# Distance bias of an attention kernel: a bias of all tiles but the first made by distance and read back skewed from memory, with a changed beginning

## The chip, the cores and the metric

The kernel runs on one core of a Trainium2 chip. The metric is the device time of one execution in microseconds (us). Its engines, by the names of the profile: PE (TensorE, matmuls; PEld its weight loads), DVE (VectorE), ACT (ScalarE), POOL (GpSimd) and SP (SyncE, which here only issues DMAs). A matmul writes to PSUM, whose buffers are the tiles of the pools ps_s, ps_t and ps_x.

## The reference

Attention with a learned distance bias, then two layers on its output, all in float32. B = 2, H = 8 heads, S = 576 positions, D = 64.

```python
scores = q @ k.T / sqrt(D)
x = log1p(abs(i - j)) / log1p(max(i, 1))        # for rows i, columns j
h = relu(x * w1 + b1)                           # 32 hidden values for every (i, j)
bias = h @ w2                                   # one value per head
attn = softmax(scores + bias)                   # over j
out = attn @ v                                  # heads side by side: 1152 x 512
y = ((out @ w_a) * (out @ w_b)) @ w_out         # 512 -> 1536 -> 512
z = y @ w_in                                    # 512 -> 1024
z = layernorm(z * softmax(z)) * g_ln
result = z @ w_out2                             # 1024 -> 512
```

## The kernel before

The attention goes over tiles of 128 rows of scores, all 576 columns at once: tiles 0 to 3 for each of the two batches, and a fifth unit that holds the last 64 rows of both batches. That makes nine units of eight heads, 72 steps. What a step does is written out in the string `ORDER`, one letter per part, at the loop near the end of the attention; `later(n, f)` and the tables `SECOND_T`, `LAST_T`, `KEYS` put other work into step n. No scheduler changes that order: each engine does its instructions as they are written. The first tile's bias is made before step 0. From about 207 us the two layers follow, which the change does not touch; some of their work already stands in the last units.

A step does, for one head: `scores` (PE, four matmuls `s<-kst,qhi` and `qlo`), `biased` (DVE, L417: adds the bias, writes `e` and the row maximum `nm`), `exp` (ACT, L424, with the row sum), `rec` (POOL, L428, then DVE, L433, its reciprocal), `shares` (POOL, L434, scales `e`), `turned` (PE transposes `e` into `pt`, L442; DVE or ACT copies it into `et`, L447 and L445) and `values` (PE, L471, into `px`). In the course of a unit Q and K for later ones are transposed (`tp_q`, `tp_k`), and split into a high and a low part (`qhi` on ACT, `qlo` on DVE, L325), as is the output (`xhi`, and `xlo` on DVE, L482).

The bias is made in 36 groups T of 16 rows. x*w1 = log1p(|i-j|)*w1/log1p(i), so one table `tabs` of log1p(distance)*w1 serves all rows: relu(a*x + b) = a*relu(x + b/a), with a = 1/log1p(i). For a group, four tiles `h` of 128 partitions (4 rows by 32 hidden values) by 576 columns are a window of the table, plus a number per partition, and no less than 0 (`bias_hidden`, L354 on DVE, L356 on ACT; which of the two is in the strings `HIDDEN`, "v" or "a"). `bias_sums` (L364) multiplies each with w2 into 32 partitions of PSUM, in two halves of 288 columns, four column groups of PE side by side. `bias_out` (L374) copies the sums (16 rows by 8 heads) with the factor a into `st`, and `bias_sent` (L383) has SP send them as rows into `bias_t`, [128 rows, 8 heads, 576]. `place(T)` gives tile and rows of T.

The table is made on PE (L209, into ps_s buffers), its right part first, the left part during the first tile's groups. `ps_s` has two buffers, shared by the table, the sums `bps` and the scores `s`. Dummy matmuls (`beside`, L405) stand in the steps 2 and 3.

Of the kernel before, what the change touches and what calls it, by code (L numbers as in the profile page):

```python
# [17 lines left out]
P = 128  # L18
# [36 lines left out]
def tile_kernel(ctx, tc, q, k, v, w1, b1, w2, w_a, w_b, w_out, w_in2, w_out2, g_ln, psi, rpsi, out):  # L55
# [14 lines left out]
    OFF = S - 4  # L70
    KD = DM // P
# [92 lines left out]
    with ExitStack() as actx:  # L164
# [7 lines left out]
        sp = actx.enter_context(tc.tile_pool(name="sp", bufs=4))  # L172
        ps_t = actx.enter_context(tc.tile_pool(name="ps_t", bufs=3, space=PSUM))
# [3 lines left out]
        tabs = ac.tile([P, UW + NG], F32, name="tabs")  # L177
        w2bd = ac.tile([P, 4 * H], F32, name="w2bd")
        rp = ac.tile([P, NG // 4], F32, name="rp")
        tb, nb = tabs[:, 0:UW], tabs[:, UW:].rearrange("p (c k) -> p c k", c=4)  # L180
        low = OFF - (S - 1 - 12)
        half = OFF - (P - 1 - 12)

        right, left, raw = (ep.tile([P, 2 * S], F32, tag="e", name=n) for n in ("psi_r", "psi_l", "raw"))
# [355 lines left out]
        for w in second[1:]:  # L540
# [3 lines left out]
            if w == second[3]:  # L544
                scores(0, 1)
# [451 lines left out]
```

## Time and profile before

| | |
|---|---|
| median of 3 runs | 546.56 us (546.26 to 547.12) |
| the profiled execution's own time | 544.4 us |
| its span in the trace | 542.6 us |
| busy: PE, DVE, ACT, POOL | 531.1, 418.9, 286.9, 156.3 us |
| first `biased` (step 0) | 28.73 us after the span's start |
| units 0 and 1 from step 3 on | 34.57 to 72.30 us |
| units 2 to 5 | 72.30 to 147.29 us |
| units 6 and 7 | 147.29 to 183.39 us |

The span is what the trace covers; the execution's time is 1.8 us more. A unit is cut at the start of its first `biased`. PE is busy nearly all of the span, in the attention with the matmuls of the scores, the bias and the values. Matmuls of four column groups run side by side, and each shows its own record, so the sum of their durations is not the time that PE spends on them; that is read from the starts of what comes before and after.

### The profile page before, as it was taken

How to read it: one execution, taken by the hardware profiler on the slowest of the kernel's cores; microseconds unless marked ns; L12 is line 12 of the kernel's file. 1: busy time of each engine (PE TensorE's matmuls, PEld its weight loads, DVE VectorE, ACT ScalarE, POOL GpSimd, SP SyncE). 2: the span in 40 equal slices, each digit the busy share in tenths (PEclk: the TensorE clock that was granted, in tenths of full speed). 3: DMA queues.
4: the chain of work that ended last, by engine and by line, in shares of the span. 5: the costliest groups of instructions: out<-in, count | busy, mean ns of one | idle time of the engine just before them, and what ended most of it. 6: DMA issues, size and time to landing. Idle time of an engine off the chain costs nothing.

```text
span 542.6 us, 12408 instructions
## 1 busy us (share of the span) xinstructions
PE 531.1 (98%) x4880; PEld 472.3 (87%) x4880; DVE 418.9 (77%) x903; ACT 286.9 (53%) x599; POOL 156.3 (29%) x262
## 2 busy tenths in 40 slices
PE   7899999999999999999999999999999999999997
PEld 3487788888878899999999999999999988888886
DVE  5788889999885795897899798897884467656661
ACT  5779987788786663555564334522534332232321
POOL 2034445555455630222222122242224330000000
PEclk9999999999999999999999999999999999999999
DMA  4895433333266012544554353444300000000011
GB/s 97 184 216 127 112 86 85 79 71 81 69 153 181 3 41 70 166 135 138 155 147 126 117 156 116 125 147 145 125 5 2 0 1 20 21 19 21 19 30 48
DMA packets 53917, 49.32 MB, mean 91 GB/s; under 512 B 31582, under 2 KB 44131, under 8 KB 53860
## 3 DMA queue, kind: packets, MB, share of 16 engines
q1 hardware_dynamic: 53584, 48.52, 33.1%
q8 instruction: 38, 0.62, 0.5%
q14 instruction: 19, 0.16, 0.1%
q10 hardware_dynamic: 276, 0.02, 0.0%
HBM read 34.37 MB, written 2.36 MB: 68 GB/s over the span
## 4 chain that ended last, share of the span: by engine, by line
PE 89%; DVE 5%; issue 2%; ACT 2%; POOL 1%; DMA 0%; SPq 0%; ACTq 0%; DVEq 0%; POOLq 0%
PE pm L132 27%; PE po L132 14%; PE py L894 9%; PE ph L834 9%; PE bps L364 7%; PE s L398 6%; PE px L471 6%; PE pt L442 5%; DVE e L417 2%; PE tp_k L288 1%; PE pl L875 1%; PE tp_q L288 1%; ACT e L424 1%; PE table L209 1%; DVE et L447 1%
## 5 line engine op out<-in xcount | busy, mean ns | idle before, releaser
L102 POOL TENSOR_SCALAR f<-f 128x512 f32<-128x512 f32 x48 | 41.2, 860 | 138.3 <-ACT f L98 128.6
L132 PE MATMUL pm<-xhi,abh 128*128 128x384 f32 x240 | 80.2, 334 | 0.0
L132 PE MATMUL pm<-xhi,abl 128*128 128x384 f32 x240 | 80.2, 334 | 0.0
L132 PE MATMUL pm<-xlo,abh 128*128 128x384 f32 x240 | 80.2, 334 | 0.0
L424 ACT ACTIVATE e<-e,nm 128x576 f32<-128x576 f32 x72 | 56.0, 778 | 29.8 <-DVE nm L417 28.4
L434 POOL TENSOR_SCALAR e<-e,rec 128x576 f32<-128x576 f32 x72 | 54.1, 751 | 28.8 <-DVE rec L433 26.7
L417 DVE CUSTOM_DVE_ANT_0 e<-s,bias 128x576 f32<-128x576 f32 x72 | 53.9, 750 | 2.4 <-PE s L398 0.8
L354 DVE TENSOR_SCALAR h<-tabs 128x576 f32<-128x576 f32 x115 | 54.6, 515 | 0.1
L151 ACT COPY one<-pm 128x384 f32<-128x384 f32 x36 | 17.3, 480 | 60.2 <-PE pm L132 60.2
L132 PE MATMUL po<-gh,oh 128*128 128x384 f32 x144 | 48.5, 337 | 0.6 <-DVE x2s L765 0.6
L364 PE MATMUL bps<-h,w2bd 128*32 128x288 f32 x576 | 46.0, 420 | 2.9 <-ACT st L374 1.6
L132 PE MATMUL po<-gh,ol 128*128 128x384 f32 x144 | 48.4, 336 | 0.0
L132 PE MATMUL po<-gl,oh 128*128 128x384 f32 x144 | 48.4, 336 | 0.0
L442 PE MATMUL pt<-ident,e 128*128 128x128 f32 x288 | 45.1, 279 | 0.9 <-POOL e L434 0.9
L132 PEld LDWEIGHTS pm<-xhi,abh 128*128 128x128 f32 x240 | 45.0, 188 | 0.0
L132 PEld LDWEIGHTS pm<-xhi,abl 128*128 128x128 f32 x240 | 45.0, 188 | 0.0
L132 PEld LDWEIGHTS pm<-xlo,abh 128*128 128x128 f32 x240 | 45.0, 188 | 0.0
L428 POOL TENSOR_SCALAR rec<-sums 128x1 f32<-128x1 f32 x72 | 21.0, 292 | 80.5 <-ACT e L424 80.2
L114 DVE SCALAR_TENSOR_TENSOR f<-words,f 128x512 int32<-128x512 int32 x48 | 42.5, 885 | 1.6
L398 PE MATMUL s<-kst,qhi 128*128 128x288 f32 x160 | 40.6, 335 | 1.2 <-DVE nm L417 1.2
L471 PE MATMUL px<-et,vsb 128*32 128x128 f32 (+1 forms) x1280 | 40.4, 264 | 0.0
L442 PEld LDWEIGHTS pt<-ident,e 128*128 128x128 f32 x288 | 32.8, 140 | 8.7 <-POOL e L434 3.7
(137 smaller groups left out, 1251.2 us busy)
## 6 DMA issues: line engine op xcount, KB each, us to landing
bias<-st SPq DMA_DIRECT2D x40, 288.0 KB, 3.6
words<-in_moe_w_out_dram SPq DMA_DIRECT2D x20, 512.0 KB, 3.6
words<-in_moe_w_a_dram SPq DMA_DIRECT2D x12, 512.0 KB, 3.7
words<-in_moe_w_b_dram SPq DMA_DIRECT2D x12, 512.0 KB, 3.5
words<-in_moe_w_in_dram SPq DMA_DIRECT2D x8, 512.0 KB, 3.7
nat_q<-in_q_dram SPq DMA_DIRECT2D x16, 128.0 KB, 3.2
arena_hi<-in_k_dram SPq DMA_DIRECT2D x16, 128.0 KB, 2.6
vsb<-in_v_dram SPq DMA_DIRECT2D x16, 128.0 KB, 2.8
```

What stands on the lines that cost most here:

```text
L114: nc.vector.scalar_tensor_tensor(out=b, in0=words[:, :, 0], scalar=29, in1=b, op0=ALU.logical_shift_right, op1=ALU.bitwise_or)
L132: nc.tensor.matmul(ps, w, x, start=(i == 0), stop=(i == n - 1))
L354: nc.vector.tensor_scalar(h, win, sc, 0.0, op0=ALU.add, op1=ALU.max)
L364: nc.tensor.matmul(bps[32 * qd:32 * qd + 32, a, 0:SH], w2bd, h[:, a * SH:(a + 1) * SH], start=True, stop=True)
L398: nc.tensor.matmul(ps[:, a, 0:SH], w, kst[:, b, h, a * SH:(a + 1) * SH], start=(m == 0), stop=(m == len(mm) - 1))
L417: nc.vector.tensor_tensor_reduce(out=halves(e), in0=ps[:, :, 0:SH], in1=halves(bias_t[it][:, h, :]), op0=ALU.add, op1=ALU.min, scale=1.0, ...
L424: nc.scalar.activation(e, e, AF.Exp, bias=nm, scale=-1.0, accum_out=sums[:, h:h + 1])
L434: nc.gpsimd.tensor_scalar(e, e, rec[:, h:h + 1], 1.0, op0=ALU.mult, op1=ALU.mult)
L442: nc.tensor.transpose(pt[:, c, :], e[:, j * TL + c * P:j * TL + (c + 1) * P], ident)
L471: nc.tensor.matmul(px[rows, p, cols], lhsT, rhs, start=(c == 0 and m == 0), stop=(c == NC), skip_group_check=True)
L834: nc.tensor.matmul(ph[u][:, a], x[:, kc, cols], w[:, kc, a * 512:(a + 1) * 512], start=(i == 0), stop=(i == 3 * KD - 1))
L894: nc.tensor.matmul(ps, x[:, c, :], w[:, c, cols], start=(i == 0), stop=(i == 3 * KF - 1))
```

## The change

The bias depends on the column only through the distance |i-j|, apart from the row's own numbers. For all groups T of 8 and up, `h` is now made over distances 0 to d-1 and no longer over columns: d = max(before + 1, behind), where before = t0 + 60 columns can lie ahead of the group's rows and behind = S - t0 behind them. d is 319 to 384 in tile 2, 381 to 448 in tile 1, 445 to 512 in tile 3, and 573 to 576 in the last one. `bias_sums` has one matmul per `h` where there were two (two if d is over 512). `bias_out` copies the sums into `st` of 636 columns in two pieces, the distances behind the row as they are and those ahead of it read backwards. SP writes `st` to a tile `bd` in memory (`bias_sent`), and one step later reads it back into `bias_t` with a skewed address pattern, four columns further to the left for each next four rows (`bias_in`, the new part "m" of a step). The first tile still has its bias made by columns, its sums split at 512 and 64 where they were 288 and 288.

The tiles are taken in the order 0, 2, 1, 3, 4. `h` of tiles 1 to 3 is all made on DVE (`HIDDEN`); before, ACT made some of it. The groups of the second tile come at other steps (`SECOND_T`), those of the later tiles two steps earlier, the last ones too (`LAST_T`). In the beginning, the second part of the table (now distances 0 to 575, 288 columns in each of two pieces) is made in ps_t buffers and no longer in ps_s, and its load `psi_l` is gone; the last two pieces of K and the Q of the second half of the heads are transposed in step 2, behind the scores of step 1; `beside` of step 2 is 2 matmuls where it was 9; the loads of V for the second batch come two steps earlier.

```diff
-ORDER = {0: "kbvioljpatsxu", 2: "kbvioljptsxu", 3: "kbglfviojptshaxu", 4: "khbvioljpatsxu", 55: "khbilospajtvxu"}
+ORDER = {0: "kbvimoljpatsxu", 2: "kbvimoljptsxu", 3: "kbglfvimojptshaxu", 4: "khbvimoljpatsxu", 55: "khbilmospajtvxu"}
...
-SECOND_T = (5, 7, 9, 10, 12, 13, 14)
-LAST_T = (48, 50, 52, 54)
-HIDDEN = (("vvva", "vvva", "vvva", "vvva", "vvva", "vvva", "vvva", "vava"),
-          ("vvvv", "avvv", "avav", "avvv", "avav", "avvv", "avav", "avvv"), ("vvvv", "avvv"))
+SECOND_T = (5, 6, 8, 9, 10, 11, 12)
+LAST_T = (46, 48, 50, 52)
+TILES = (0, 2, 1, 3, 4)
+HIDDEN = (("vvva", "vvva", "vvva", "vvva", "vvva", "vvva", "vvva", "vvva"),
+          ("vvvv",), ("vvvv",), ("vvvv",), ("vvvv", "avvv"))
...
+        dp = actx.enter_context(tc.tile_pool(name="dp", bufs=4, space=bass.MemoryType.DRAM))
...
-        def table(a, n, row, at):
-            ps = ps_s.tile([P, 2, 512], F32, tag="s", name=f"table_{a}")
+        def table(n, at, step, pool, tag):
             w = (n + 1) // 2
+            halves = []
             for i in range(2):
                 m = min(w, n - i * w)
+                ps = pool.tile([P, 512], F32, tag=tag, name=f"table_{step}_{i}")
                 for g in range(4):
-                    o = a + i * w - 4 * g - at
-                    nc.tensor.matmul(ps[g * HID:(g + 1) * HID, i, 0:m], w1r, row[:, o:o + m], start=True, stop=True)
-            return [(tb[:, a + i * w:a + min(n, (i + 1) * w)], ps[:, i, 0:min(w, n - i * w)]) for i in range(2)]
-        halves_r = table(half, UW - half, psi_r, half - 12)
+                    o = at + i * w - step * g
+                    nc.tensor.matmul(ps[g * HID:(g + 1) * HID, 0:m], w1r, psi_d[:, o:o + m], start=True, stop=True)
+                halves.append((tb[:, i * w:i * w + m], ps[:, 0:m]))
+            return halves
+        halves = table(NX, 12, 4, ps_s, "s")
...
+        def reach(T):
+            _, it, r, c = place(T)
+            t0 = it * P + r + c
+            return t0 + 60, S - t0
         def bias_hidden(T, quads=range(4)):
-            it, r, c = place(T)
+            n, it, r, c = place(T)
+            before, behind = reach(T)
             for qd in quads:
                 t0 = it * P + r + 16 * qd
-                h = hp.tile([P, S], F32, tag="h", name=f"h_{T}_{qd}")
-                win = tb[:, OFF - t0 - c:OFF - t0 - c + S]
+                a, d = (OFF - half - t0 - c, S) if n == 0 else (0, max(before + 1, behind))
+                h = hp.tile([P, S], F32, tag="h", name=f"h_{T}_{qd}")[:, 0:d]
+                win = tb[:, a:a + d]
                 sc = nb[:, c, t0 // 16:t0 // 16 + 1]
-                if HIDDEN[min(it, 2)][T % len(HIDDEN[min(it, 2)])][qd] == "v":
+                if HIDDEN[n][T % len(HIDDEN[n])][qd] == "v":
                     nc.vector.tensor_scalar(h, win, sc, 0.0, op0=ALU.add, op1=ALU.max)
                 else:
                     nc.scalar.activation(h, win, AF.Relu, bias=sc)
...
         def bias_sums(T):
-            bps = ps_s.tile([P, 2, 512], F32, tag="s", name=f"bps_{T}")
+            bps = ps_s.tile([P, 2, 512], F32, tag="s", name=f"bps_{T}").rearrange("p a j -> p (a j)")
             for qd, h in enumerate(bias_w[T]):
-                for a in range(2):
-                    nc.tensor.matmul(bps[32 * qd:32 * qd + 32, a, 0:SH], w2bd, h[:, a * SH:(a + 1) * SH], start=True, stop=True)
+                d = h.shape[1]
+                for a in range(0, d, 512):
+                    cols = slice(a, min(d, a + 512))
+                    nc.tensor.matmul(bps[32 * qd:32 * qd + 32, cols], w2bd, h[:, cols], start=True, stop=True)
             bias_w[T] = bps
-        def bias_out(T, send=True):
-            it, r, c = place(T)
+        def bias_rows(T):
+            _, it, r, c = place(T)
             if it not in bias_t:
                 bias_t[it] = big.tile([P, H, S], F32, tag="big", name=f"bias_{it}")
-            st = stp.tile([P, S], F32, tag="st", name=f"st_{T}")
+            return [bias_t[it][base + c:base + 64:4] for base in ((r,) if it < NC else (0, TL))]
+        def bias_out(T, send=True):
+            n, it, r, c = place(T)
+            before, behind = reach(T)
+            st = stp.tile([P, W], F32, tag="st", name=f"st_{T}")
+            bps = bias_w.pop(T)
             k = 9 * c + 2 * it + r // 64
-            nc.scalar.activation(st.rearrange("p (a j) -> p a j", a=2), bias_w.pop(T)[:, :, 0:SH], AF.Copy, scale=rp[:, k:k + 1])
+            if n == 0:
+                nc.scalar.activation(st[:, 0:S], bps[:, 0:S], AF.Copy, scale=rp[:, k:k + 1])
+                for rows in bias_rows(T):
+                    nc.sync.dma_start(rows, st[:, 0:S])
+                return
+            nc.scalar.activation(st[:, before:W], bps[:, 0:behind], AF.Copy, scale=rp[:, k:k + 1])
+            nc.scalar.activation(st[:, 0:before], bps[:, before:0:-1], AF.Copy, scale=rp[:, k:k + 1])
             bias_w[T] = st
             if send:
                 bias_sent(T)
         def bias_sent(T):
-            it, r, c = place(T)
-            st = bias_w.pop(T)
-            for base in ((r,) if it < NC else (0, TL)):
-                nc.sync.dma_start(bias_t[it][base + c:base + 64:4], st)
+            st, bias_w[T] = bias_w[T], dp.tile([P, W], F32, tag="bd", name=f"bd_{T}")
+            nc.sync.dma_start(bias_w[T], st)
+        def bias_in(T):
+            bd = bias_w.pop(T)[:, :]
+            for rows in bias_rows(T):
+                nc.sync.dma_start(rows, bass.AP(bd.tensor, bd.offset + 60, [[8 * W - 4, 16], [W, 8], [1, S]]))
...
-        units = [(it, [b]) for it in range(NC) for b in range(B)] + [(NC, list(range(B)))]
+        units = [(it, [b]) for it in TILES[:NC] for b in range(B)] + [(TILES[NC], list(range(B)))]
...
-        nc.sync.dma_start(psi_l, psi[3:4, low + 3 - 12:half + 3])
...
-                halves_l = table(low, half - low, psi_l, low - 12)
+                halves = table(S, 12 + OFF - half, 0, ps_t, "t")
...
-            turn(w)
-            keep_high(w)
-            if w == second[3]:
-                scores(0, 1)
-        later(2, beside, 9)
+            if w in second[:4]:
+                turn(w)
+                keep_high(w)
+        scores(0, 1)
+        for w in second[4:] + second[:1]:
+            later(2, turn, w)
+            keep_at.setdefault(3, []).append(w)
+        later(2, beside, 2)
         later(3, beside, 3)
+        later(3, keep_low, second[0])
         later(1, bias_sent, N0)
-        later(1, turn, second[0])
-        later(2, keep_high, second[0])
-        low_at[3] = [second[0]]
+        in_at[4] = [N0]
...
-            later(7 + p, load_v, 1, p)
+            later(5 + p, load_v, 1, p)
...
-            n = LAST_T[r] if i == NC - 1 else 16 * i + (SECOND_T[r - 1] if i == 0 else 2 * r)
+            n = LAST_T[r] if i == NC - 1 else SECOND_T[r - 1] if i == 0 else 16 * i - 2 + 2 * r
...
+            in_at.setdefault(n + 2, []).append(T)
...
+                if part == "m":
+                    for T in in_at.get(n, []):
+                        bias_in(T)
```

The rows below are the programs' instructions in their order, engine by engine, with the names that the code gives and a buffer number. First SP in units 0 and 1, the queue that issues the DMAs, before; `bias_1` is the bias of the second tile, T = 11 to 15:

```order
L383 DMA bias_1_422<-st_11_898 16x8x576
L334 DMA vsb_161<-in_v_dram 128x4x64 x2
L383 DMA bias_1_422<-st_12_978 16x8x576
L383 DMA bias_1_422<-st_13_1084 16x8x576
L257 DMA nat_q_2_1_0_1102<-in_q_dram 128x4x64
L383 DMA bias_1_422<-st_14_1121 16x8x576
L383 DMA bias_1_422<-st_15_1188 16x8x576
```

And the same groups after, where `bd` is the tile in memory and `bias_2` the bias of the tile that is now the second:

```order
L410 DMA bd_11_866<-st_11_863 128x636
L263 DMA nat_q_2_0_0_891<-in_q_dram 128x4x64
L416 DMA bias_2_560<-bd_11_866 16x8x576
L410 DMA bd_12_915<-st_12_912 128x636
L416 DMA bias_2_560<-bd_12_915 16x8x576
L410 DMA bd_13_996<-st_13_993 128x636
L416 DMA bias_2_560<-bd_13_996 16x8x576
L410 DMA bd_14_1045<-st_14_1042 128x636
L416 DMA bias_2_560<-bd_14_1045 16x8x576
L410 DMA bd_15_1104<-st_15_1101 128x636
L263 DMA nat_q_2_1_0_1121<-in_q_dram 128x4x64
L416 DMA bias_2_560<-bd_15_1104 16x8x576
```

Each group now has two DMAs on SP, and the next group's write stands behind the read of this one.

Next DVE in unit 2, around the step that also has `xlo` of the unit ahead, before:

```order
L417 ISA nm_2_3_1390 128x1
L482 TENSOR_TENSOR xlo_1021<-px_1_801,xhi_1020 128x4x128
L447 COPY et_2_1_1401<-pt_2_1_1396 128x512
L354 TENSOR_SCALAR h_19_1_1414<-tabs_104 128x576
L433 RECIPROCAL rec_2_1229<-rec_2_1229 128x1
L417 ISA e_2_4_1427,nm_2_4_1428<-s_2_4_1407,bias_1_422 128x576
L417 ISA nm_2_4_1428 128x1
L354 TENSOR_SCALAR h_19_2_1470<-tabs_104 128x576
L354 TENSOR_SCALAR h_19_3_1472<-tabs_104 128x576
```

And after:

```order
L450 ISA nm_2_3_1394 128x1
L515 TENSOR_TENSOR xlo_1039<-px_1_806,xhi_1038 128x4x128
L480 COPY et_2_1_1406<-pt_2_1_1401 128x512
L368 TENSOR_SCALAR h_20_0_1417<-tabs_106 128x384
L368 TENSOR_SCALAR h_20_1_1419<-tabs_106 128x384
L466 RECIPROCAL rec_2_1237<-rec_2_1237 128x1
L450 ISA e_2_4_1428,nm_2_4_1429<-s_2_4_1412,bias_2_560 128x576
L450 ISA nm_2_4_1429 128x1
L368 TENSOR_SCALAR h_20_2_1473<-tabs_106 128x384
L368 TENSOR_SCALAR h_20_3_1475<-tabs_106 128x384
```

Every step has two `h` there now, of fewer columns, where some steps had one; and the group is one further on.

Last PE in the beginning, from the table's second part on, before:

```order
L209 MATMUL table_9_344<-psi_l_108,psi_r_107 32x224 x8
L364 MATMUL bps_5_353<-h_5_0_308,w2bd_105 32x288 x2
L364 MATMUL bps_5_353<-h_5_1_310,w2bd_105 32x288 x2
...
L398 MATMUL s_0_1_457<-kst_160,qhi_0_0_0_213 128x288 x2
L398 MATMUL s_0_1_457<-kst_160,qlo_0_0_0_214 128x288 x2
L288 MATMUL tp_k_0_1_3_464<-ident_72,arena_lo_164 128x128 x4
L288 MATMUL tp_k_0_1_4_472<-ident_72,arena_lo_164 128x64 x4
L288 MATMUL tp_q_0_1_0_502<-ident_72,nat_q_0_1_0_182 128x128 x4
L398 MATMUL s_0_2_512<-kst_160,qhi_0_0_0_213 128x288 x2
```

And after:

```order
L214 MATMUL table_0_0_346<-logs_109 32x288 x4
L214 MATMUL table_0_1_351<-logs_109 32x288 x4
L380 MATMUL bps_5_356<-h_5_0_310,w2bd_107 32x512
L380 MATMUL bps_5_356<-h_5_0_310,w2bd_107 32x64
...
L431 MATMUL s_0_1_460<-kst_163,qhi_0_0_0_215 128x288 x2
L431 MATMUL s_0_1_460<-kst_163,qlo_0_0_0_216 128x288 x2
L431 MATMUL s_0_2_495<-kst_163,qhi_0_0_0_215 128x288 x2
L431 MATMUL s_0_2_495<-kst_163,qlo_0_0_0_216 128x288 x2
L294 MATMUL tp_k_0_1_3_500<-ident_72,arena_lo_167 128x128 x4
L294 MATMUL tp_k_0_1_4_505<-ident_72,arena_lo_167 128x64 x4
L294 MATMUL tp_q_0_1_0_510<-ident_72,nat_q_0_1_0_184 128x128 x4
```

The table has 288 columns in place of 224, the sums are split at 512, and two pieces of K and the Q stand behind the scores of step 2.

## Rows read from the trace of the kernel before

**Rows 1.** The page: the span, and busy time by engine.
```profile
span 542.6 us, 12408 instructions
...
PE 531.1 (98%) x4880; PEld 472.3 (87%) x4880; DVE 418.9 (77%) x903; ACT 286.9 (53%) x599; POOL 156.3 (29%) x262
```

**Rows 2.** Busy time by stretch, with granted clock and DMA share.
```profile
core 0: us, PE busy (x) PEld busy (x) DVE busy (x) ACT busy (x) POOL busy (x), PEclk, DMA share, GB/s
34.57:72.30 37.73, 37.55 (x544) 29.34 (x546) 33.26 (x93) 32.25 (x70) 14.69 (x30) 1.00 0.57 130
72.30:90.78 18.48, 18.48 (x300) 15.45 (x296) 17.22 (x45) 14.85 (x34) 9.36 (x18) 1.00 0.34 81
90.78:109.66 18.88, 18.88 (x321) 15.92 (x316) 17.32 (x46) 15.35 (x34) 9.63 (x19) 1.00 0.33 78
...
128.14:147.29 19.15, 19.03 (x323) 16.02 (x318) 17.29 (x46) 15.30 (x34) 9.62 (x19) 1.00 0.33 77
147.29:166.43 19.14, 18.35 (x279) 15.27 (x270) 15.07 (x41) 14.67 (x33) 8.75 (x18) 1.00 0.63 146
```

**Rows 3.** Timeline of PE: start, duration, operation, tiles, and number of records.
```profile
89.59 1.20 PE L364 MATMUL bps<-h,w2bd 128*32 128x288 f32 x16
90.59 1.08 PE L471 MATMUL px<-et,vsb 128*32 128x128 f32 x32
```

**Rows 4.** Timeline of a step with a copy and two `h`.
```profile
93.04 0.76 DVE L417 CUSTOM_DVE_ANT_0 e<-s,bias 128x576 f32<-128x576 f32 x1
...
93.73 0.69 DVE L447 COPY et<-pt 128x512 f32<-128x512 f32 x1
...
93.84 0.78 ACT L424 ACTIVATE e<-e,nm 128x576 f32<-128x576 f32 x1 [0.69 <-DVE nm L417]
...
94.33 0.94 DVE L354 TENSOR_SCALAR h<-tabs 128x576 f32<-128x576 f32 x2
...
94.79 0.52 POOL L428 TENSOR_SCALAR rec<-sums 128x1 f32<-128x1 f32 x1 [0.74 <-ACT e L424]
...
95.47 0.76 DVE L417 CUSTOM_DVE_ANT_0 e<-s,bias 128x576 f32<-128x576 f32 x1
```

**Rows 5.** Timeline of a step of unit 7, which makes no bias.
```profile
170.62 0.74 DVE L417 CUSTOM_DVE_ANT_0 e<-s,bias 128x576 f32<-128x576 f32 x1
...
172.41 0.19 POOL L428 TENSOR_SCALAR rec<-sums 128x1 f32<-128x1 f32 x1 [0.58 <-ACT e L424]
...
172.75 0.76 DVE L417 CUSTOM_DVE_ANT_0 e<-s,bias 128x576 f32<-128x576 f32 x1
```

**Rows 6.** Instructions by line and form up to 208 us.
```profile
line engine op names shapes xcount | busy us, mean ns | idle before us <-releasers
L354 DVE TENSOR_SCALAR h<-tabs 128x576 f32<-128x576 f32 x115 | 54.6, 515 | 0.1
...
L275 DVE TENSOR_SCALAR arena_lo<-arena_hi 128x256 fp32r<-128x256 f32 x8 | 2.3, 284 | 0.0
L102 DVE TENSOR_SCALAR single<-single 128x512 f32<-128x512 f32 x4 | 1.7, 416 | 0.0
```

**Rows 7.** Timeline of the beginning; idle time before in brackets.
```profile
17.25 0.96 PE L209 MATMUL table<-psi_l,psi_r 1*32 1x224 f32 x16
...
20.27 1.20 PE L364 MATMUL bps<-h,w2bd 128*32 128x288 f32 x16 [0.55 <-ACT st L374]
...
22.50 1.20 PE L364 MATMUL bps<-h,w2bd 128*32 128x288 f32 x16 [1.03 <-ACT st L374]
...
23.80 0.74 ACT L374 ACTIVATE st<-bps,rp 128x576 f32<-128x576 f32 x1 [1.11 <-PE bps L364]
...
28.73 0.76 DVE L417 CUSTOM_DVE_ANT_0 e<-s,bias 128x576 f32<-128x576 f32 x1 [0.39 <-DMA arena_hi<-in_k_dram]
```

**Rows 8.** Timeline: `biased` of the steps 9 and 16.
```profile
51.79 0.74 DVE L417 CUSTOM_DVE_ANT_0 e<-s,bias 128x576 f32<-128x576 f32 x1
...
72.30 0.76 DVE L417 CUSTOM_DVE_ANT_0 e<-s,bias 128x576 f32<-128x576 f32 x1 [0.25 <-PE bps L364]
```

**Rows 9.** DMA issues: KB each, median us from issue to landing.
```profile
bias<-st SPq DMA_DIRECT2D x40, 288.0 KB, 3.6
...
out_dram<-osb SPq DMA_DIRECT2D x7, 256.0 KB, 2.0
```

More of the change, by code (lines that the diff above doesn't have):

```diff
@@ L70, in tile_kernel @@
     OFF = S - 4
+    W = S + 60
     KD = DM // P
@@ L172, in tile_kernel @@
         sp = actx.enter_context(tc.tile_pool(name="sp", bufs=4))
+        dp = actx.enter_context(tc.tile_pool(name="dp", bufs=4, space=bass.MemoryType.DRAM))
         ps_t = actx.enter_context(tc.tile_pool(name="ps_t", bufs=3, space=PSUM))
         ps_x = actx.enter_context(tc.tile_pool(name="ps_x", bufs=1, space=PSUM))
-        tabs = ac.tile([P, UW + NG], F32, name="tabs")
+        half = OFF - (P - 1 - 12)
+        NX = UW - half
+        tabs = ac.tile([P, NX + NG], F32, name="tabs")
         w2bd = ac.tile([P, 4 * H], F32, name="w2bd")
         rp = ac.tile([P, NG // 4], F32, name="rp")
[L180 to L184, printed above, removed]
+        tb, nb = tabs[:, 0:NX], tabs[:, NX:].rearrange("p (c k) -> p c k", c=4)
+        logs, at_i, raw = (ep.tile([P, 2 * S], F32, tag="e", name=n) for n in ("logs", "psi_i", "raw"))
         w2r, rp_in = raw[:, 0:H], raw[:, H:H + NG // 4]
-        nr_, nl_ = UW - half + 12, half - low + 12
-        psi_r, w1r, b1r = (right[0:1, o:o + n] for o, n in ((0, nr_), (nr_, HID), (nr_ + HID, HID)))
-        psi_l, psi_i = left[0:1, 0:nl_], left[0:1, nl_:nl_ + 4 * NG].rearrange("p (c t) -> p c t", c=4)
+        psi_d, w1r, b1r = (logs[0:1, o:o + n] for o, n in ((0, NX + 12), (NX + 12, HID), (NX + 12 + HID, HID)))
+        psi_i = at_i[0:1, 0:4 * NG].rearrange("p (c t) -> p c t", c=4)
         warm = ac.tile([P, 1], F32, name="warm")
-        nc.sync.dma_start(psi_r, psi[0:1, half - 12:UW])
+        nc.sync.dma_start(psi_d, psi[0:1, half - 12:UW])
         nc.sync.dma_start(w1r, w1)
@@ L215, in tile_kernel @@
             nc.tensor.matmul(ps_nb[g * HID:(g + 1) * HID], b1r, psi_i[:, :, g::4], start=True, stop=True)
-        nc.scalar.copy(*halves_r[0])
+        nc.scalar.copy(*halves[0])
         nc.vector.tensor_copy(nb, ps_nb)
-        nc.vector.tensor_copy(*halves_r[1])
+        nc.vector.tensor_copy(*halves[1])
         for g in range(4):
@@ L482, in inputs_low @@
             nc.vector.tensor_tensor(out=xlo, in0=px, in1=xhi.bitcast(F32), op=ALU.subtract)
-        units = [(it, [b]) for it in range(NC) for b in range(B)] + [(NC, list(range(B)))]
+        units = [(it, [b]) for it in TILES[:NC] for b in range(B)] + [(TILES[NC], list(range(B)))]
         qs = {}
-        extra, sums_at, out_at, keep_at, low_at = {}, {}, {}, {}, {}
+        extra, sums_at, out_at, in_at, keep_at, low_at = {}, {}, {}, {}, {}, {}
         def later(n, f, *args):
@@ L515, in tile_kernel @@
             if T == N0:
-                nc.scalar.copy(*halves_l[0])
-                nc.vector.tensor_copy(*halves_l[1])
+                nc.scalar.copy(*halves[0])
+                nc.vector.tensor_copy(*halves[1])
             if T <= N0:
@@ L633, in tile_kernel @@
             for part in ORDER[max(i for i in ORDER if i <= n)]:
-                if part == "o":
+                if part == "m":
+                    for T in in_at.get(n, []):
+                        bias_in(T)
+                elif part == "o":
                     for T in out_at.get(n, []):
```

4 lines of the change are left out of this document (2 added, 2 removed).

## The prediction

> **What bounds the kernel now.** I read the page first: TensorE is busy 531.1 of 542.6 us [rows 1]. That share does not say what a removed TensorE instruction is worth, so I cut the attention, which is all the change touches, into its units of eight steps at the starts of `biased`, and read the busy time by stretch [rows 2]. In the units from 72.30 to 128.14 TensorE is busy all of the time, while VectorE has 17.2 of 18.5 us and ScalarE 15. Then I read one step in order of time. A step's softmax is a ring that runs once per step: VectorE adds the bias and takes the row maximum, ScalarE takes the exponential, GpSimd turns the sum, VectorE inverts it, and only then comes the next `biased`. With nothing in the way that ring takes 172.75 - 170.62 = 2.13 us [rows 5]. Where VectorE has a copy of `et` and two `h` to do, the ring is longer: the copy starts at 93.73, the two `h` at 94.33, they end at 95.27, and GpSimd's small `rec`, ready at 94.79, takes 0.52 there in place of 0.19 and ends 0.04 behind them; the next `biased` starts at 95.47, a step of 2.43 [rows 4]. So the reader is to see two chains of nearly one length: TensorE's sum of work and this ring. Work taken from TensorE alone gives at most what the ring also gives back.
>
> The ring and TensorE don't bound the beginning; there the bias of the first tile does. The sums of T = 6 and 7 wait 0.55 and 1.03 us for ScalarE to free a buffer, the copy of T = 7 starts at 23.80, and the first `biased` at 28.73, when its bias rows have landed [rows 7].
>
> **The change part by part.** All against the profiled execution's 544.4 us (span 542.6). The median of the three runs shown is 546.56, 2.2 above it; the sum of differences is carried over to the median.
>
> *Widths of `h`.* One `h` of 576 columns has an interval of 0.94 - 0.51 = 0.43 behind another [rows 4, 6]. The mean duration is 515 ns at 576, and of the same form 416 at 512 (L102) and 284 at 256 (L275) [rows 6]. The last two give 0.52 ns per column, so I take intervals of 0.295 us at 320 columns, 0.327 at 383, 0.36 at 447 and 0.393 at 510. The form is the same, tensor_scalar on VectorE, so both ends are near.
>
> *Widths of the sums.* Sixteen matmuls of 288 columns, four column groups side by side, keep TensorE from 89.59 until the next kind of work starts at 90.59 [rows 3]: 1.0, of which I take 0.97 as paid by columns, 1.68 ns for each of 576. One matmul of d columns in each group then costs 0.54 (d = 319), 0.64 (382), 0.75 (447) and 0.86 (510). No row shows a matmul of 320 to 512 columns in this form; the bounds are proportional to columns (these) and no gain (0.97).
>
> *A, the beginning.* The table's second half takes no ps_s buffer any more, so the waits of 0.55 and 1.03 go; the table itself grows from 224 to 288 columns, 0.96 to about 1.23 [rows 7]. Net 1.3 us earlier at T = 7's copy. The first two steps also lose transposes of K that now come in step 2; 0.2 for them. A: -1.5. Bounds: -0.3 (the DMA queue, which brings K in the same stretch, keeps the landing where it is) and -2.2.
>
> *B, units 0 and 1 from 34.57 to 72.30.* TensorE: T = 9 to 15 fall from 7 x 0.97 = 6.79 to 4.19, -2.6; T = 17's sums come into this stretch, +0.75; fewer changes of kind, -0.2: -2.05. VectorE: 23 `h` of 0.43 were here, 9.9 us (ScalarE made 10 more); after it 38 stand here, 12 of 0.295, 16 of 0.328, 10 of 0.36: 12.4. That is +2.5 on an engine that has 4.5 us idle in 37.73 [rows 2]. TensorE gives 2.05, VectorE may take it all; I take half, -1.0, with 0 and -2.05 as bounds.
>
> *C, units 2 to 5.* By the step of [rows 4], 1.29 until the first `h`, two intervals, 0.28 to the next `biased`: 2.43 before, and 2.29 (d = 447), 2.22 (383) and 2.36 (510) after. A unit has five such steps, two of the bare ring, 2.13, and one in which VectorE does `xlo` and `et`, 2.38 before with one `h`, and with two now 2.62 to 2.75. Before: 5 x 2.43 + 4.26 + 2.38 = 18.8, against 18.48 and 18.88 in the rows. After, units 2 and 3: 5 x 2.255 + 4.26 + 2.68 = 18.2 each, -1.0 for both. Units 4 and 5: 5 x 2.325 + 4.26 + 2.7 = 18.6, nothing off 18.48, and off 19.15 between 0.2 (if the 0.35 by which it stands above 18.8 stays) and 0.55; I take -0.4. C: -1.4. TensorE's sums alone would give -3.5 here.
>
> *D, unit 6.* The last tile's groups come two steps earlier, which can take something of TensorE's 0.79 idle in 19.14 [rows 2]; I take -0.3 between 0 and -0.8.
>
> *What I cost at nothing.* The copy of the sums in two parts: ScalarE has over 3 us idle per unit, and loses the `h` it made in most tiles. The removed load of psi: its place on SP is before anything waits. The 90% more bytes of bias: the DMA share is 0.33 to 0.57 in these units [rows 2]. From the last unit on nothing changes.
>
> *The trip through memory.* A tile's rows are written out, and a step later read back. On SP the read waits until the write has landed, and all that is queued behind it waits with it: the next T's write, the loads of Q and V. The second tile's bias is needed at step 16. From T = 11 on the groups follow each other by a step, so the last read leaves SP five writes and some 2.4 us of issue after T = 11's write and lands one read later: 6L + 2.4, if each leg takes L. From step 9 to step 16 there are 72.30 - 51.79 = 20.5 us [rows 8], less the 1.5 that B may take out of these steps at most, 19.1. It breaks even at L = 2.8. No row shows either leg. Nearest are 256 KB from SBUF to memory, 2.0, and the same bias rows from SBUF to SBUF, 288 KB, 3.6 [rows 9]. The write is nearest to the first, so I take the chain as just hidden, 0, with a bound of +4.9 (L = 3.6).
>
> The Trainium skill has a rule on this, "DMA: Bandwidth & Descriptors", section "Anatomy of one DMA — SWDGE (gpsimd) path": about 2.0 us fixed for each DMA, mostly the receipt of the last write and longest when the target is HBM, and the bytes at 436 GB/s. By it the write would take 2.75 us and the read 2.68, an estimate from that page, and the chain 18.8 us, just hidden; the row of 3.6 us for 288 KB says that the page's 2.7 is too low for the bias rows, and no run here shows the other leg yet.
>
> **Sum.** -1.5 - 1.0 - 1.4 - 0.3 = -4.2: 540.2 profiled, 542.3 as a median.
>
> **The rivals.** *TensorE's sum rules.* The sums fall by 6.1 us in all (2.6 for T = 9 to 15, 2.2 for 16 to 23, 1.3 for 24 to 31), the changes of kind by 0.2, the beginning by 1.7: 538.5. For it: TensorE has no idle time in these units [rows 2]. Against: the ring's own 2.43 [rows 4]. Chance 0.16.
>
> *The ring and VectorE take everything but the beginning.* 19 `h` move from ScalarE to VectorE; if the step with `xlo` and the steps that had one `h` lose what the others gain, only A is left: 545.0, or 546.3 if A is at its lower bound. For it: VectorE's 17.2 of 18.5. Against: each `h` is a quarter shorter. Chance 0.20, half of it over 0.2% faster.
>
> *The second tile's bias is late at step 16*, the other side. At L = 3.6 it is 4.9 late: 547.2; at 4.1 it is 7.9 late: 550. Slower than before from both legs of 3.7. For it: the row of 3.6, for the same rows. Against: writes to memory land in 2.0. Chance 0.22: 0.03 faster, 0.09 the same, 0.10 slower.
>
> **How the numbers follow.** My forecast has 0.42, with a range of its own of 541 to 544. A measurement of this kernel can tell 0.2%, 1.1 us, from no change. Faster: 0.42 + 0.16 + 0.10 + 0.03 = 0.71; the same: 0.08 + 0.09 = 0.17; slower: 0.02 + 0.10 = 0.12. The range reaches down to the first rival and up to the third at L = 3.6: 538.3 to 547.5.
>
> **What would show it.** In the profile after: the copy of T = 7 at about 22.5 and the first `biased` at 27.4 (A); the sums of a tile at 0.54 to 0.86 by width; steps with a copy and two `h` at 2.22 to 2.36 and `rec` still ending behind the second `h` (C); units 2 and 3 at about 18.2. I'm wrong if TensorE stays without idle time in the units and they fall by 1 us each (first rival), if they stay at 18.5 to 18.9 (second), or if `biased` of step 16 waits for a DMA and that step is longer than 2.5 us (third).

## The result, and the profile after

| | before | after |
|---|---|---|
| median | 546.41 us of 4 runs | 554.35 us of 4 runs (553.46 to 554.95) |
| ratio to before | | 1.0146, 95% interval 1.0129 to 1.0163 |
| profiled execution, span | 544.4, 542.6 us | 554.33, 552.0 us |

The kernel became 1.5% slower, where 0.8% faster was forecast; it lies 7 us above the upper end of the range. Slower is the side that the third rival had forecast.

The page of the kernel after, span, busy time and two kinds of DMA (KB each, median us to landing), beside [rows 1, 9]:

```profile
span 552.0 us, 12101 instructions
...
PE 529.5 (96%) x4681; PEld 465.1 (84%) x4681; DVE 418.3 (76%) x922; ACT 279.5 (51%) x608; POOL 155.2 (28%) x262
...
bias<-bd SPq DMA_DIRECT2D x32, 288.0 KB, 3.9
bd<-st SPq DMA_DIRECT2D x28, 318.0 KB, 3.8
```

TensorE is busy for 1.6 us less, and the span is 9.4 longer. The profiled execution of the kernel before was 2.0 us under that kernel's median, the one after at its median; so the 9.4 us, and the stretches below, stand against 7.9 us by the medians. The busy time by stretch of the kernel after, cut at the starts of `biased` as in [rows 2]; columns as there:

```profile
35.10:70.30 35.20, 32.67 (x457) 25.41 (x455) 33.03 (x100) 27.59 (x66) 13.40 (x27) 1.00 0.71 172
70.30:81.50 11.20, 4.46 (x68) 3.40 (x65) 2.29 (x8) 1.96 (x5) 1.88 (x3) 0.83 0.57 164
81.50:101.30 19.80, 18.39 (x243) 13.98 (x247) 16.67 (x48) 14.05 (x35) 7.98 (x17) 0.84 0.49 141
101.30:119.80 18.50, 18.04 (x284) 14.52 (x280) 16.83 (x49) 14.50 (x37) 9.07 (x19) 1.00 0.52 153
119.80:138.50 18.70, 18.23 (x270) 14.09 (x261) 17.33 (x48) 14.21 (x36) 9.25 (x18) 1.00 0.51 147
138.50:158.00 19.50, 18.96 (x301) 14.79 (x296) 17.61 (x48) 15.19 (x37) 9.18 (x19) 1.00 0.52 144
158.00:175.90 17.90, 17.40 (x256) 14.32 (x251) 13.52 (x37) 13.62 (x33) 8.14 (x18) 1.00 0.63 170
```

The second row is one step, the 15th, and every engine stands still in it. It takes 11.2 us where it took 2.4, so 8.8 of the 9.4 us are there. The others: 0.5 until step 3 (35.07 after 34.57), -0.1 from there to step 15, +1.3 in unit 2 (19.8 after 18.48, at a granted clock of 0.84), +0.2 in units 3 to 5 together (56.7 after 56.5), and -1.2 in unit 6 (17.9 after 19.14).

VectorE around that step; the wait is in brackets. The profile puts it down to a write, `bd<-st`, that landed at about the same time; what `biased` reads is the bias tile, which the read of the tile's last group fills:

```profile
72.46 0.16 DVE L466 RECIPROCAL rec<-rec 128x1 f32<-128x1 f32 x1
81.45 0.76 DVE L450 CUSTOM_DVE_ANT_0 e<-s,bias 128x576 f32<-128x576 f32 x1 [8.82 <-DMA bd<-st]
```

This is the `biased` of step 16, the first that needs the second tile's bias. SP in that time, T = 13 to 15 (each row an issue; the read `bias<-bd` waits for its write to land):

```profile
68.19 0.54 SPq L416 DMA_DIRECT2D bias<-bd  x1
68.82 1.07 SPq L410 DMA_DIRECT2D bd<-st  x1
72.64 0.54 SPq L416 DMA_DIRECT2D bias<-bd  x1
73.27 0.54 SPq L410 DMA_DIRECT2D bd<-st  x1
73.91 0.38 SPq L263 DMA_DIRECT2D nat_q<-in_q_dram  x1
77.14 0.54 SPq L416 DMA_DIRECT2D bias<-bd  x1
```

Write, 3.8 us of waiting, read, next write: one group in 4.5 us, where a step takes 2.3. The read of T = 15, the last of the tile, goes out at 77.14, and `biased` starts 4.3 us later.

TensorE stands still from 74.8 to 82.3, and comes back at half rate; rows of TensorE after the wait and later, the sums of one group each:

```profile
82.27 0.85 PE L431 MATMUL s<-kst,qhi 128*128 128x288 f32 x2 [7.45 <-DVE nm L450]
...
85.03 1.72 PE L380 MATMUL bps<-h,w2bd 128*32 128x446 f32 x8
...
90.61 0.95 PE L380 MATMUL bps<-h,w2bd 128*32 128x445 f32 x8
```

### The profile page after: what moved, and what is told of

Its sections match the earlier page's. It is cut to its first block, busy times and chain, and to the rows that moved or that the text cites. A ratio compares the mean times of both kernels' runs of the same rounds, so it can differ in the third digit from the quotient of the medians.

```text
span 552.0 us, 12101 instructions
## 1 busy us (share of the span) xinstructions
PE 529.5 (96%) x4681; PEld 465.1 (84%) x4681; DVE 418.3 (76%) x922; ACT 279.5 (51%) x608; POOL 155.2 (28%) x262
## 4 chain that ended last, share of the span: by engine, by line
PE 69%; DVE 6%; issue 4%; ACT 4%; DMA 4%; POOL 1%; SPq 0%; ACTq 0%; POOLq 0%; DVEq 0%
PE pm L135 26%; PE po L135 11%; PE py L932 9%; PE ph L872 9%; PE px L504 4%; DMA bd<-st 3%; PE pt L475 3%; PE s L431 3%; PE bps L380 2%; DVE e L450 2%; PE pl L913 1%; ACT e L457 1%; PE tp_q L294 1%; POOL rec L461 1%; DVE f L117 1%
## 5 line engine op out<-in xcount | busy, mean ns | idle before, releaser
L105 POOL TENSOR_SCALAR f<-f 128x512 f32<-128x512 f32 x48 | 42.6, 887 | 137.0 <-ACT f L101 128.9
L450 DVE CUSTOM_DVE_ANT_0 e<-s,bias 128x576 f32<-128x576 f32 x72 | 54.0, 751 | 11.2 <-DMA bd<-st 8.8
L368 DVE TENSOR_SCALAR h<-tabs 128x576 f32<-128x576 f32 (+17 forms) x134 | 54.6, 455 | 2.0 <-PE bps L380 1.4
L504 PEld LDWEIGHTS px<-et,vsb 128*32 128x32 f32 x1280 | 34.3, 111 | 13.2 <-issue 7.4
L380 PE MATMUL bps<-h,w2bd 128*32 128x512 f32 (+17 forms) x384 | 40.7, 498 | 3.6 <-DVE nm L450 1.8
L461 POOL TENSOR_SCALAR rec<-sums 128x1 f32<-128x1 f32 x72 | 18.7, 260 | 89.1 <-ACT e L457 88.9
```

The costliest lines, as they stand in the source:

```text
L380: nc.tensor.matmul(bps[32 * qd:32 * qd + 32, cols], w2bd, h[:, cols], start=True, stop=True)
L450: nc.vector.tensor_tensor_reduce(out=halves(e), in0=ps[:, :, 0:SH], in1=halves(bias_t[it][:, h, :]), op0=ALU.add, op1=ALU.min, scale=1.0, ...
L504: nc.tensor.matmul(px[rows, p, cols], lhsT, rhs, start=(c == 0 and m == 0), stop=(c == NC), skip_group_check=True)
```

## The experiments

Two theories stood against each other. The first is the third rival: the trip through memory, in SP's order, makes the second tile's bias late, and the rest of the change is a small gain. The second: the changed work itself is slower, by what VectorE took over, and the wait only stands where another would.

**The write ahead of the read.** Two letters of a step's parts change places, nothing else: a step sends the newer group's write first and then waits for the older one's.

```diff
-ORDER = {0: "kbvimoljpatsxu", ...
+ORDER = {0: "kbviomljpatsxu", ...
```

> In each step the write of the newer group goes out on SP ahead of the read of the older one, so that a read's wait for its write no longer holds up the next write. Theory (the wait of step 16 is SP's queue: write, wait, read, one group at a time, 4.5 us per group): the read of T = 15 leaves SP at about 72 us in place of 77.1, the wait of step 16 falls from 8.8 to about 3.7 us, and TensorE is idle for less: 547.5 to 549 us. Rival (the DMA engines themselves are full in that stretch, their share is 1.0 from 75 to 77 us, and the order of issue changes nothing): the wait stays over 7.5 us and the time over 553 us.

Measured: 543.36 us against 545.64 of before, ratio 0.9956 (0.9939 to 0.9973). 10 to 11 us under the changed kernel, and faster than before by 2.3 us. SP in this kernel, the reads of T = 11 to 15:

```profile
57.33 0.55 SPq L416 DMA_DIRECT2D bias<-bd  x1
57.97 0.76 SPq L410 DMA_DIRECT2D bd<-st  x1
58.83 0.55 SPq L416 DMA_DIRECT2D bias<-bd  x1
61.38 0.33 SPq L410 DMA_DIRECT2D bd<-st  x1
61.85 0.54 SPq L416 DMA_DIRECT2D bias<-bd  x1
63.34 0.32 SPq L410 DMA_DIRECT2D bd<-st  x1
64.31 0.54 SPq L416 DMA_DIRECT2D bias<-bd  x1
64.94 0.54 SPq L263 DMA_DIRECT2D nat_q<-in_q_dram  x1
66.61 0.54 SPq L416 DMA_DIRECT2D bias<-bd  x1
```

From T = 12 on the reads follow each other at the steps' pace, 1.5 to 3.0 us. The last read goes out at 66.61, 10.5 us earlier than in the kernel after and 5 earlier than I expected, since no write is held up any more; the step 15 takes 2.5. So the wait was the queue's order, not the engines that move the data, though their share is up to 1.0 there.

**No trip.** The rows go straight from `st` to the bias tile; the skew, and with it the right bias, is left out.

```diff
...
-            nc.sync.dma_start(bias_w[T], st)
...
+            for rows in bias_rows(T):
+                nc.sync.dma_start(rows, st[:, 60:60 + S])
...
```

> The trip through memory is left out: each group's columns 60 to 635 go straight from st to the bias tile, as the kernel before sends them, without the skew, so the bias of the later tiles is wrong by columns; all other work is that of the changed kernel. Theory (the trip costs the wait of step 16, 8.8 us, and by the idle time the slower clock of some 1.8 us after it, and the rest of the change is a small gain): about 543.7 us, no wait at step 16, TensorE at its full clock from 14 us on. Rival (the changed work itself is slower, on VectorE above all, and the wait at step 16 only stands where another would): 548 us or more.

Measured: 543.45 us, ratio 0.9958 (0.9943 to 0.9972). That is the time of the kernel ahead: with the write first, the trip costs nothing that can be told, and the second theory falls.

**The first tile's sums in halves**, 288 and 288 columns in place of 512 and 64, for the beginning:

```diff
...
+                w = SH if T < P // 16 else 512
...
```

> The first tile's sums are split 288 and 288 columns as in the kernel before, in place of 512 and 64. In the changed kernel TensorE's rows run at half rate until 12.7 us, before until 9.8 us, which costs 1.45 us at T = 1's sums. Theory (the split decides when the rate rises): full rate from about 9.8 us, T = 7's copy 1.2 to 1.5 us earlier at about 22.8 us, the first biased at about 27.7 us; the time falls by 0.9 to 1.4 us to 553.0 to 553.5, since the queue of writes and reads starts earlier too. Rival (the rate rises late for another reason, such as the order of the first work): full rate at 12.7 us again and 554.3 us.

Measured: 552.65 us, ratio 1.0134 (1.0111 to 1.0156), no different from the 1.0146 of the kernel after. In the profiled execution TensorE's rows are at half rate until 12.6 us again, and T = 7's copy starts at 24.00. It is the slowest of the four (554.8; the others 552.4 to 552.7), and no row shows when the rate rose in the others. That the split alone does not decide is shown from the other side too: three later kernels with 512 and 64 columns have the full rate from about 10 us.

**TensorE kept busy in the wait**, by 56 dummy matmuls of 7.5 us:

```diff
...
+        later(17, fill, 56)
```

> 56 dummy matmuls of 288 columns stand on TensorE ahead of the scores that wait at step 16, so that TensorE is busy for some 7 us of the wait; nothing else is changed. Theory (the idle time takes TensorE's clock to half rate, from 82.3 to 88 us, and that costs unit 2 1.3 to 1.8 us): granted clock 1.00 from 81.5 to 101 us, unit 2 in 18.3 us in place of 19.8, 552.6 us in all. Rival (the ring hides the slow clock and unit 2 is long for another reason): 554.3 us.

Measured: 551.33 to 556.24 us in four runs, ratio 1.0143 (1.0106 to 1.0180). Inconclusive. In the profiled execution the dummies end at 81.1, the bias comes at 82.8, and the granted clock falls to 0.50 all the same, at about 83.6; the other three runs show a mean clock of 1.00, and their median, 552.9, is 1.4 under that of the kernel after, about what the theory gives; but they spread over 2.7 us. What the clock costs is read from rows alone: unit 2 takes 19.8 us at 0.84 in the kernel after, and 18.3 at 1.00 in the kernel with the write first, 1.5 us. All of it stands in the unit's third step, 3.76 us in place of 2.29; the `biased` behind it waits for scores that stand behind TensorE's work at half rate. The size varies: unit 2 took 19.1 us in the profiled execution of the kernel with the halves, and 20.3 in this one.

All that follow are built on the kernel with the write first; the next four ask why it gained 2.3 us and not 4.2.

**One `h` of the step with `xlo` on ScalarE**:

```diff
-          ("vvvv",), ("vvvv",), ("vvvv",), ("vvvv", "avvv"))
+          ("vvvv",), ("avvv", "vvvv", "vvvv", "vvvv"), ("avvv", "vvvv", "vvvv", "vvvv"), ("vvvv", "avvv"))
```

> Built on the kernel with the write ahead of the read (2.3 us faster than before); in the three steps with xlo of the units 2 to 4 one of VectorE's two h (T = 20, 24, 28) is made on ScalarE (and one of T = 16). Theory (units 2 to 5 gain nothing because the step with xlo, et and two h, 2.68 to 2.74 us, gives back what the shorter steps of 2.22 to 2.36 gain): that step falls to some 2.35 in units 2, 3 and 4, 0.35 each, and the time is 3.1 to 3.5 us under that of before. Rival (ScalarE, which now has two copies per group, makes exp late, and the step stays over 2.6): 2.3 us under that of before or less.

Measured: 543.01 against 545.69, ratio 0.9949 (0.9935 to 0.9962): 2.7 us. VectorE in that step of unit 3, the kernel after first, then this one:

```profile
107.89 0.76 DVE L450 CUSTOM_DVE_ANT_0 e<-s,bias 128x576 f32<-128x576 f32 x1
108.57 0.69 DVE L515 TENSOR_TENSOR xlo<-px,xhi 128x512 fp32r<-128x512 f32 x1
109.17 0.68 DVE L480 COPY et<-pt 128x512 f32<-128x512 f32 x1
109.77 0.81 DVE L368 TENSOR_SCALAR h<-tabs 128x445 f32<-128x445 f32 x2
...
110.56 0.74 DVE L450 CUSTOM_DVE_ANT_0 e<-s,bias 128x576 f32<-128x576 f32 x1
```

```profile
96.62 0.76 DVE L450 CUSTOM_DVE_ANT_0 e<-s,bias 128x576 f32<-128x576 f32 x1
97.30 0.69 DVE L515 TENSOR_TENSOR xlo<-px,xhi 128x512 fp32r<-128x512 f32 x1
97.91 0.68 DVE L480 COPY et<-pt 128x512 f32<-128x512 f32 x1
98.50 0.45 DVE L368 TENSOR_SCALAR h<-tabs 128x445 f32<-128x445 f32 x1
...
98.94 0.74 DVE L450 CUSTOM_DVE_ANT_0 e<-s,bias 128x576 f32<-128x576 f32 x1
```

The step falls from 2.67 to 2.32, and by about as much in units 2 and 4. Units 2 and 3 gain 0.5 and 0.3; unit 4 does not, as another step of it is 0.4 longer. So VectorE does set that step. In the whole time the two kernels' intervals overlap.

**Both on ScalarE** ("aavv" in the two places):

> As the one ahead, but with both h of that step on ScalarE. Theory (VectorE alone sets that step): it falls to 2.1 us, 0.6 each, and the time is 3.8 to 4.2 us under that of before. Rival (two h of 0.65 on ScalarE make the exponential of the next step late): that step or the next stays 0.3 us longer, 3.3 us under or less.

Measured: 543.96 us, ratio 0.9968 (0.9955 to 0.9980), 1.7 us under before. The step falls to 2.1, and the next one rises to between 2.8 and 3.0. In unit 3 ScalarE makes two `h` (1.22 us) and two copies ahead of the next exponential, which starts at 100.22, 0.8 late. The rival's mechanism, and more of it than I gave.

**One `h` of four of T = 9 to 15 on ScalarE**:

```diff
-          ("vvvv",), ("vvvv",), ("vvvv",), ("vvvv", "avvv"))
+          ("vvvv",) + 7 * ("avvv",), ("vvvv",), ("vvvv",), ("vvvv", "avvv"))
```

> Built on the kernel with the write ahead of the read; of T = 9 to 15 one h of four is made on ScalarE, the others on VectorE. Theory (units 0 and 1 gain nothing because VectorE sets them, busy 35.2 of the 37.6 us from step 3 to 16: it now makes all h and the sums' 2.6 us saved on TensorE become idle time): VectorE loses 7 h of 0.31, and the stretch falls from 37.6 to 36 us or so; 3.5 to 4.3 us under before. Rival (the ring or the loads of K and V set it): 37.3 us or more, 2.3 us under before.

Measured: 542.21 us, ratio 0.9941 (0.9925 to 0.9956), the fastest median here; its interval overlaps that of the kernel with the write first. The stretch that it was made for did not move: 37.6 us from step 3 to 16, with VectorE down from 35.2 to 33.8. Steps 3 to 9 get 0.3 shorter, the later ones as much longer. By the stretch the rival is right. Step by step both are: the steps 3, 6 and 7 fall from 3.18, 3.23 and 3.32 to 2.88, 2.93 and 3.17, but step 8 rises from 2.99 to 3.33 and step 9 stays at 4.54. In these two VectorE, relieved, waits for TensorE: in step 8 for the sums of a group, in step 9 for K's transpose (0.49 us with the write first).

```profile
51.27 0.42 DVE L368 TENSOR_SCALAR h<-tabs 128x383 f32<-128x383 f32 x1 [0.74 <-PE bps L380]
...
53.82 0.29 DVE L281 TENSOR_SCALAR nat_k<-arena_hi 128x256 fp32r<-128x256 f32 x1 [0.79 <-PE tp_k L294]
```

That TensorE's work would have to come earlier there too is argued from these rows, and no run tried it. The first three steps take 5.7 us in place of 6.0, which is part of what this kernel gains.

**K turned where it was before**, ahead of the scores of step 2:

```diff
-            if w in second[:4]:
-                turn(w)
-                keep_high(w)
-        scores(0, 1)
...
+            turn(w)
+            keep_high(w)
+            if w == second[3]:
+                scores(0, 1)
...
```

> Built on the kernel with the write ahead of the read; the last two pieces of K and the second Q are turned where they were before (ahead of the scores of step 2, with 9 dummy matmuls in step 2). Theory (TensorE waits for the bias from 28.4 to 29.9 us, and turning K in step 2 only puts 1.65 us of matmuls on the first steps' path): from the first biased to that of step 3 5.8 us as before, in place of 6.0, and 0.2 to 0.5 us off the whole. Rival (the place of these matmuls is free, or their move is worth something): no change or up to 0.6 us longer.

Measured: 544.03 us, ratio 0.9968 (0.9955 to 0.9980). The first three steps take 5.7 us in place of 6.0, as the theory has it, and step 3 to 16 takes 38.3 in place of 37.6: given back. The whole is not shorter.

**The loads of V two steps later**, on the kernel with the write first, and **both edits of `HIDDEN` together**, without and with these loads:

```diff
-            later(5 + p, load_v, 1, p)
+            later(7 + p, load_v, 1, p)
```

> Built on the kernel with the write ahead of the read; the loads of V of the second batch stand two steps later, as before. Theory A (VectorE sets the steps 3 to 9, busy 15.0 of 15.2 us there): the place of these loads changes nothing, the stretch from step 3 to 16 stays at 37.6 us and the time 2.3 us under before. Theory B (the DMA engines, whose share is 1.0 to 1.15 from step 8 to 10, bring Q, K and the bias late): the stretch falls by 0.5 us or more.

> Built on the kernel with the write ahead of the read; one h of four of T = 9 to 15 and one h in the three steps with xlo are made on ScalarE: the two edits tried one by one, together. If both work apart from each other, the step with xlo is at 2.3 us in units 2 to 4 and the time 3.7 to 4.2 us under before, the fastest so far; if ScalarE is then the limit, 3.2 us or less.

> As the one ahead, with the loads of V two steps later as before. Theory A: no difference from it. Theory B (with VectorE relieved the full DMA engines set the steps 8 and 9, 3.4 and 4.5 us): these two steps fall by 0.5 us or more together, and the time to 4.2 to 4.7 us under before.

Measured: the loads alone 543.83 (0.9960, 0.9948 to 0.9972), no change; both edits 542.45 (0.9948, 0.9931 to 0.9965); with the loads 542.72 (0.9949, 0.9932 to 0.9966). The runs of these last two spread over 3.0 and 4.3 us. Steps 8 and 9 stay at 3.3 and 4.5 in both, so the place of these loads is not it. The two edits don't add up. One reason is in the rows of VectorE in the kernel with both, at the start of unit 4:

```profile
105.09 0.76 DVE L450 CUSTOM_DVE_ANT_0 e<-s,bias 128x576 f32<-128x576 f32 x1
...
108.11 0.76 DVE L450 CUSTOM_DVE_ANT_0 e<-s,bias 128x576 f32<-128x576 f32 x1 [0.69 <-DMA bias<-bd]
```

Its last read went out at 104.02 and landed 4.1 us later: with the steps shorter, the trip is late again at the next tile.

## Why the prediction was wrong

**The step that failed is the one on the trip through memory**: "It breaks even at L = 2.8 ... The write is nearest to the first, so I take the chain as just hidden, 0". The form 6L + 2.4 was nearly right: with five writes of the measured 3.8 and a read of 3.9 it gives 25.3, and from the write of T = 11 (55.09) to the landing of T = 15's read (81.4) it was 26.3. Two of its numbers were not. The write has nearly the bytes, and the direction, of the kernel's output [rows 9], but lands in 3.8 us and not 2.0, like the bias rows that move within SBUF; I took the nearest row by kind of target, where the nearest by place in the program was the better one. Part of the difference goes with the read beside it: a write of the chain leaves 0.6 us after a read, while in unit 2 the writes of 87.78 and 92.60 us left 1.4 and 1.8 after one, and the reads that wait for them went out 3.0 and 2.8 us later. What makes up the rest was not tested. And the time available was not 19.1 but 17.5: without the wait `biased` of step 16 would start at 72.6, and T = 11's write did not leave SP at the start of step 9 (53.45) but 1.6 us later, behind the read of T = 10 and loads of V, though ScalarE had copied its sums out by 50.3. The queue was late before the chain that I counted began. 26.3 - 17.5 is the 8.8 of the wait. With the one order exchanged, the cost that I took, 0, is right: the fault was not that a trip was made, but that the read stood ahead of the next group's write. The price of the wait is larger than its length, as TensorE's clock fell in it (1.5 us in unit 2 of this execution); no case of mine had that.

The range's upper end came from L = 3.6 of [rows 9]; with both legs at the 4.1 that I named in the rival, it gave 550. The rest is the beginning and the units 0 to 5, which did not gain what I took off for them, and the clock.

The rule that I cited from the Trainium skill, "DMA: Bandwidth & Descriptors", section "Anatomy of one DMA — SWDGE (gpsimd) path", gave 2.75 and 2.68 us for the two legs; these runs measure 3.8 and 3.9. That section is about transfers that GpSimd issues, which my prediction passed over; these were issued from SP. The measurement decides: the chain is hidden by that rule and is not on the chip.

**The beginning** (-1.5 forecast, +0.5 measured until step 3). The waits of 0.55 and 1.03 us [rows 7] are gone: the sums of T = 6 and 7 stand as one piece. But TensorE ran at half rate until 12.7 us in this execution, and until 9.8 in that of before; rows of the kernel after:

```profile
9.87 1.12 PE L294 MATMUL tp_q<-ident,nat_q 128*128 128x128 f32 x4
10.92 2.13 PE L380 MATMUL bps<-h,w2bd 128*32 128x512 f32 x16
...
21.32 2.75 PE L380 MATMUL bps<-h,w2bd 128*32 128x512 f32 x32
...
24.11 0.74 ACT L398 ACTIVATE st<-bps,rp 128x576 f32<-128x576 f32 x1 [0.33 <-PE bps L380]
```

The first two rows take 0.66 and 1.20 at full rate. Among this kernel and the later ones the half rate ends between 9.8 and 12.7, and the first `biased` lies between 27.4 and 29.1, earliest where the rate rises earliest. At 27.4 (both `h` on ScalarE, full rate from 9.8) it is where I had forecast it. So the term's first part was right for an execution with an early rise; its last 0.2 was not: the second step is 0.3 us shorter than before, but the third 0.5 longer.

**Units 0 and 1** (-1.0 forecast). The steps 3 to 9 and 10 to 15 by stretch, and unit 2, with the write first; under them the same steps before:

```profile
34.30:57.10 22.80, 21.05 (x298) 16.17 (x297) 22.00 (x70) 17.28 (x41) 7.78 (x16) 1.00 0.90 218
57.10:71.90 14.80, 14.00 (x209) 10.88 (x211) 13.21 (x38) 12.00 (x30) 6.92 (x14) 1.00 0.70 200
71.90:90.20 18.30, 17.81 (x271) 14.09 (x264) 16.60 (x47) 14.16 (x35) 8.76 (x18) 1.00 0.55 153
```

```profile
34.57:55.69 21.12, 21.12 (x301) 16.58 (x303) 19.31 (x56) 17.86 (x40) 8.00 (x16) 1.00 0.68 147
55.69:72.30 16.61, 16.43 (x254) 12.77 (x247) 13.95 (x39) 14.39 (x32) 6.69 (x14) 1.00 0.44 108
```

The later steps get 1.8 us shorter, and the steps 3 to 9 1.7 longer; in these VectorE is busy 22.0 of 22.8 us. They cancel, which was one bound of the term. The price of the sums was right: 445 columns keep TensorE from 90.61 to 91.38 us, 0.77, where I had 0.75 for 447. That the 1.7 us are VectorE's load is shown in part only: with one `h` of four on ScalarE three of these steps got shorter, and the stretch did not.

**Units 2 to 5** (-1.4 forecast, 0 measured with the write first, 75.0 us both). The step's form held to 0.01 in most steps: 2.29 at 447 columns, 2.22 at 381, 2.36 at 510; with `xlo` it is 2.61 to 2.81, where I had 2.62 to 2.75. Rows of the kernel after in unit 4, beside [rows 4]:

```profile
121.95 0.76 DVE L450 CUSTOM_DVE_ANT_0 e<-s,bias 128x576 f32<-128x576 f32 x1
...
122.64 0.69 DVE L480 COPY et<-pt 128x512 f32<-128x512 f32 x1
...
123.24 0.81 DVE L368 TENSOR_SCALAR h<-tabs 128x448 f32<-128x448 f32 x2
...
123.70 0.39 POOL L461 TENSOR_SCALAR rec<-sums 128x1 f32<-128x1 f32 x1 [0.69 <-ACT e L457]
...
124.25 0.76 DVE L450 CUSTOM_DVE_ANT_0 e<-s,bias 128x576 f32<-128x576 f32 x1
```

`rec` again ends with the second `h` and not before. What was off is the count, and single steps. I took five steps with a copy and two `h` in every unit before. The units 2 and 4 had four, since ScalarE made some `h`, and after there are five; unit 4 so went from 18.48 to 18.7. In unit 5 one step takes 2.9, where ScalarE's own `h` of T = 33, the split of Q and two copies delay the exponential by 0.8. The last steps of units 3 and 5 take 2.52 and 2.65 with the write first, 2.39 before; the kernel without the trip has them at 2.61 and 2.75, so it is not the trip, and the cause is open.

**Unit 6** (-0.3 forecast): -1.2 in the kernel after, beyond my bound of -0.8, and -0.9 with the write first; the direction was right.

**The other rivals.** TensorE's sum does not rule: TensorE has idle time in every unit after, and its saved columns gave nothing where the ring was. For the units 2 to 5 the second rival was right: with the write first, the ring and VectorE take what the shorter steps gain; what is left there comes from the beginning and unit 6.

## What to carry to other kernels

When a transfer becomes two that wait for each other, write out the queue's order for consecutive pieces: if the second leg stands ahead of the next piece's first leg, the pieces go one by one, and the pace is a leg's latency, not its bytes. Put the next first leg ahead of the waiting second one. Take a leg's latency from transfers that run in the same stretch, and leave room beyond the length of a wait for what TensorE's clock loses in it.

## What the runs showed of the hardware

- TensorE was idle from 74.8 to 82.3 us; its granted clock was 1.00 (2.4 GHz) until 77.5 and 0.50 (1.2 GHz) from 78 to nearly 88, 5.7 us after the work had come back. A group's sums took 1.72 us in place of 0.95 in it.
- At the start of a run TensorE's rows are at half rate although the granted clock is shown as 1.00, and the end of that differs from execution to execution, 9.8 to 12.7 us with the same instructions there. T = 7's copy starts between 22.7 and 24.1 with it, and the first `biased` between 27.4 and 29.1, a spread as large as the term that was forecast for the beginning. The Trainium skill says in "TensorE: Matmul & The Clock Gate", Part 1, that the point of the rise differs from run to run of one kernel; these traces agree, but their spread of 2.9 us is wider than the 500 ns either way that it gives.
- A write of 318 KB to memory took 3.8 us to land and a read of 288 KB 3.9, also at 73 to 81 us where nothing else of size was under way but one of each and a load of Q. Writes that left 1.4 to 1.8 us after the read ahead of them, and not 0.6, had landed after 2.8 to 3.0 us. The output's 256 KB at the end took 2.0.
